# Chunked attention and a squared-ReLU feed-forward on one core: stores on the GpSimd queue, loads of two groups issued ahead of them, and a first block that starts in halves

## The chip, the cores and the metric

The kernel runs on one core of a Trainium2 chip. The metric is the device time of one execution in microseconds (us). A core has five engines with instruction streams of their own: TensorE (PE in the profile; its weight loads are PEld), VectorE (DVE), ScalarE (ACT), GpSimd (POOL) and SyncE (SP). Each takes its instructions strictly in order, and a DMA is issued by an instruction on one of these streams ("SPq", "ACTq", "POOLq" in the profile), so a DMA that must wait holds up everything behind it on that engine.

## The reference

Queries, keys and values have the shape 8 batches x 8 heads x 576 tokens x 64. Attention is computed inside chunks of 64 tokens; its output, laid out as 4608 tokens x 512, goes through a feed-forward with 2048 hidden units.

```
scores = scale * q_c @ k_c^T                   # within each chunk of 64 tokens
attn   = exp(scores - max) / (sum + 1e-9)
x      = (attn @ v_c) as [4608, 512]           # heads side by side
h      = maximum(x @ w_in, 0)                  # [4608, 2048]
out    = (h * h) @ w_out                       # [4608, 512], float32
```

## The kernel before

**Groups and blocks.** The 4608 tokens form 18 groups of 256 tokens; two groups make a block of 512. The blocks are [0, 1], [3, 2], [4, 5], ..., [16, 17] (line 41). The feed-forward works through a block at a time, and the attention of later groups is woven into it.

**One block of feed-forward.** `ffn_in` (L305) runs over 16 tiles `ft` of 128 hidden units. For each it makes four matmuls into a PSUM bank of the ring `ps_ffn` (four banks, L52), a ReLU on ACT (L318) and a square on DVE (L319) into `gT`. `ffn_out` (L323) then makes, for each of four tiles of 128 tokens, 16 matmuls into a `ps_ffn` bank, copies the bank to `o_sb` on ACT (L345) and stores 256 KB to `out` (L346). Block 0 uses `ffn_out_by_ft` (L350) instead, which takes hidden tiles in the outer loop so that it can follow the arrival of `w_out`; its stores are at L373. The very last tile is stored in two halves by ACT and SP (L340).

**Attention of one group**, by the names in the plan: the transposes of q and k (on PE through PSUM for groups 0 to 3: T, and TE for the first two; from group 4 on a cast to bf16 on POOL, C, L216, followed by a DMA transpose on SP's queue, TD, L223); the scores and their exponential (SC, L237 and L244); the product with the values and the division (AV, L260, L267, L268); and the transpose of the result to `xT`, which feeds `ffn_in` (XT: on PE for groups under 6, L287 and L291, by DMA on SP's queue after that, L281). SC, AV, XT and the PE transposes take their PSUM from the ring `ps_att` (two tiles of two banks each, L53). In T, q and k share one such tile: DVE copies the q half, ACT the k half (L173).

**The order is written out by hand.** The schedule is manual: each engine executes its instructions in the order of the program text. Each block has a table of slots (L411 to L445). A slot is one `yield` of `ffn_in` (one `ft`) or of `ffn_out` (four `ft`). At a slot, one piece of the coming loads may be issued on SP, and then the steps planned for it. A slot places an instruction between others of its own engine; it is not a point in time. Loads of q and k are at L102 and L110, of v at L117 and L124, of the weights at L136 and L144 (five staging buffers, each freed by a cast on POOL, L139 and L147). All of them run on SP's queue, but for the first `w_in` load, which ACT issues. A DMA on SP or ACT takes a completion semaphore out of a small rotating set, and waits until the earlier DMA on that semaphore has landed.

**The start** (L382 to L399). After the loads of groups 0 and 1 the order on PE is: transposes of 0, scores of 0, transposes of 1, values of 0, scores of 1, `xT` of 0, values of 1, `xT` of 1, with 46 filler matmuls in between (`keep_busy`, L207). Then come the weight loads and the loads of groups 3 and 2, and block 0's `ffn_in` over all 512 columns.

**Blocks 0 to 2.** Block 0 issues no loads in its slots (L417). Block 1 issues the loads of groups 4 and 5 in slots 0 to 16, then C of 4 and 5 at slots 22 and 26, TD at 27 and 31, then the q and k loads of groups 6 and 7 from slot 34; the scores of 4 and 5 are at slot 37. After the last slot of block 1, C and TD of groups 6 and 7 follow (L457 to L460). Block 2 makes the scores of 6 and 7 at slot 6, and block 3 those of 8 and 9 at slot 8.

Of the kernel before, what the change touches and what calls it, by code (L numbers as in the profile page):

```python
# [17 lines left out]
def kernel(  # L18
# [9 lines left out]
    nc = tc.nc  # L28
# [143 lines left out]
        for t in range(2):  # L172
            copy(out=dst[:, t], in_=src[:, t])  # L173

    def transpose_qk(g):
        ps = ps_att.tile([128, 1024], FP32, name="ps_att").bitcast(BF16)
        qkT = att_pool.tile([128, 2, 2, n_hp, 128], BF16, name="qkT", bufs=4)
        state["qkT", g] = qkT
        for which in range(2):
            transpose_paired(g, which, ps[:, which * 1024:(which + 1) * 1024])  # L180
        for which, copy in enumerate((nc.vector.tensor_copy, nc.scalar.copy)):
            copy_paired(copy, qkT[:, which], ps[:, which * 1024:(which + 1) * 1024])

    def transpose_qk_early(g, k_copy):
        qkT = att_pool.tile([128, 2, 2, n_hp, 128], BF16, name="qkT", bufs=4)
        state["qkT", g] = qkT
        for which, copy in enumerate((nc.vector.tensor_copy, k_copy)):
            bank = ps_ffn.tile([128, 512], FP32, name="ps_ffn").bitcast(BF16)
            transpose_paired(g, which, bank)
            copy_paired(copy, qkT[:, which], bank)  # L190

# [52 lines left out]
        nc.scalar.activation(  # L244
            out=e.rearrange("p a h t q -> p (a h t q)"), in_=ps, func=AF.Exp, scale=scale)

    def values(g):
        e = state.pop(("e", g))
        veb = v_even[g % NV].bitcast(BF16)
        vob = [v_odd[(2 * g + n) % NO].bitcast(BF16) for n in range(3)]  # L250
        x = att_pool.tile([128, 2, n_hp, 2, D], BF16, name="x", bufs=3)
        state["x", g] = x
        for t in range(2):
            ps = ps_att.tile([128, 2, 512], FP32, name="ps_att")
            for hp in range(n_hp):
                for a in range(2):
                    for p in range(2):
                        c = p ^ a
                        vb = vob[t + p] if a else veb[:, t]
                        nc.tensor.matmul(  # L260
                            out=ps[64 * p:64 * p + 64, a, hp * (D + 1):(hp + 1) * (D + 1)],
                            lhsT=e[64 * c:64 * c + 64, a, hp, t, :],
                            rhs=vb[64 * c:64 * c + 64, hp, 1::2],
                            start=True, stop=True)
            o = ps[:, :, 0:n_hp * (D + 1)].rearrange("p a (h d) -> p a h d", d=D + 1)
            rec = att_pool.tile([128, 2, n_hp], FP32, name="rec", bufs=4)
            nc.vector.reciprocal(out=rec, in_=o[:, :, :, D])  # L267
            nc.vector.tensor_tensor(  # L268
                out=x[:, t].rearrange("p h a d -> p a h d"),
                in0=o[:, :, :, 0:D],  # L270
                in1=rec.to_broadcast([128, 2, n_hp, D]),
                op=ALU.mult)
# [17 lines left out]
                    identity=ident)  # L290
        nc.vector.tensor_copy(out=dst, in_=psb)  # L291

    T, C, TD = transpose_qk, cast_qk, transpose_qk_dma
    SC, AV, XT = scores, values, transpose_x

    def TE(g):
        transpose_qk_early(g, nc.scalar.copy)

    def XE(g):
        for t in range(2):  # L300
            transpose_x_early(g, t)

    gTs = {}

    def ffn_in(j, c, n):  # L305
        if j not in gTs:
            gTs[j] = ffn_pool.tile([128, n_ft, BT], BF16, name="gT")
        gT, xT = gTs[j], xTs[j]
        for ft in range(n_ft):
            h = ps_ffn.tile([128, 512], FP32, name="ps_ffn")  # L310
            for dt in range(n_dt):
                nc.tensor.matmul(  # L312
                    out=h[:, 0:n],
                    lhsT=w_in_bf[:, dt, ft * 128:(ft + 1) * 128],
                    rhs=xT[:, c // 128:(c + n) // 128, dt, :],
                    start=(dt == 0), stop=(dt == n_dt - 1))
            rl = ffn_pool.tile([128, 512], BF16, name="rl", bufs=3)
            nc.scalar.activation(out=rl[:, 0:n], in_=h[:, 0:n], func=AF.Relu)  # L318
            nc.vector.tensor_tensor(  # L319
                out=gT[:, ft, c:c + n], in0=rl[:, 0:n], in1=rl[:, 0:n], op=ALU.mult)  # L320
            yield

    def ffn_out(j):  # L323
        gT = gTs.pop(j)
        for tt in range(len(blocks[j]) * GT // 128):
            o_ps = ps_ffn.tile([128, d_model], FP32, name="ps_ffn")
            for ft in range(n_ft):
                nc.tensor.matmul(  # L328
                    out=o_ps,
                    lhsT=gT[:, ft, tt * 128:(tt + 1) * 128],  # L330
                    rhs=w_out_bf[:, ft, :],
                    start=(ft == 0), stop=(ft == n_ft - 1))
                if ft == n_ft - 1:
                    t0 = blocks[j][tt // 2] * GT + tt % 2 * 128
                    if j == len(blocks) - 1 and tt == 2 * len(blocks[j]) - 1:
                        for copy, dma, c in ((nc.scalar.copy, nc.scalar, 0),
                                             (nc.vector.tensor_copy, nc.sync, 256)):
                            o_sb = ffn_pool.tile([128, d_model], FP32, name="o_sb", bufs=4)
                            copy(out=o_sb[:, 0:256], in_=o_ps[:, c:c + 256])
                            dma.dma_start(  # L340
                                out=out[t0:t0 + 128, c:c + 256], in_=o_sb[:, 0:256])
                        yield
                        continue
                    o_sb = ffn_pool.tile([128, d_model], FP32, name="o_sb", bufs=4)
                    nc.scalar.copy(out=o_sb, in_=o_ps)  # L345
                    nc.scalar.dma_start(out=out[t0:t0 + 128, :], in_=o_sb)  # L346
                if ft % 4 == 3:
                    yield

    def ffn_out_by_ft(j):  # L350

        gT = gTs.pop(j)
        n_tt = len(blocks[j]) * GT // 128
        o_ps = [ps_ffn.tile([128, d_model], FP32, name="ps_ffn") for _ in range(n_tt)]

        def mm(tt, ft):
            nc.tensor.matmul(  # L357
                out=o_ps[tt],
                lhsT=gT[:, ft, tt * 128:(tt + 1) * 128],
                rhs=w_out_bf[:, ft, :],  # L360
                start=(ft == 0), stop=(ft == n_ft - 1))

        for ft in range(n_ft - 4):
            for tt in range(n_tt):
                mm(tt, ft)
            yield
        for tt in range(n_tt):
            for ft in range(n_ft - 4, n_ft):
                mm(tt, ft)
            o_sb = ffn_pool.tile([128, d_model], FP32, name="o_sb", bufs=4)  # L370
            nc.scalar.copy(out=o_sb, in_=o_ps[tt])
            t0 = blocks[j][tt // 2] * GT + tt % 2 * 128
            nc.scalar.dma_start(out=out[t0:t0 + 128, :], in_=o_sb)  # L373
            yield

    def pieces(grps):
# [3 lines left out]
            yield from v_pieces(g)  # L380

    go(pieces([0, 1]))  # L382
    transpose_qk_early(0, nc.scalar.copy)
    keep_busy(8)
    SC(0)
    keep_busy(6)
    transpose_qk_early(1, nc.scalar.copy)
    load_w_in(0, nc.scalar, 2)
    AV(0)
    SC(1)  # L390
    keep_busy(8)
    XE(0)
    keep_busy(8)
    AV(1)
    keep_busy(8)
    transpose_x_early(1, 0)
    keep_busy(4)
    transpose_x_early(1, 1)
    keep_busy(4)  # L399

    for i in range(1, 8):
        load_w_in(i)
# [5 lines left out]
    for j, grps in enumerate(blocks):  # L408
# [5 lines left out]
            plan.setdefault(slot, []).append((f, g))  # L414

        if j == 0:
            loads, go_slots = iter(()), []  # L417
            for slot, f in ((24, T), (27, SC), (29, AV), (31, XT)):
                at(slot, f, nxt[0])
            at(31, T, nxt[1])  # L420
            phases = [ffn_in(0, 0, 512), ffn_out_by_ft(0)]
        elif j == 1:
            go_slots = [*range(17), *range(34, 48)]
            loads = itertools.chain(pieces(nxt), *map(qk_pieces, far))
            for slot, f in ((4, SC), (8, AV), (12, XT)):
                at(slot, f, grps[1])
            for i, g in enumerate(nxt):
                for slot, f in ((22 + 4 * i, C), (27 + 4 * i, TD), (37, SC), (39 + 2 * i, AV),
                                (42 + 2 * i, XT)):
                    at(slot, f, g)  # L430
            phases = [ffn_in(1, 0, 256), ffn_in(1, 256, 256), ffn_out(1)]
        else:
            loads, go_slots = pieces(far), range(32)
            slots = {SC: 8, AV: 11, XT: 15, C: 14, TD: 19}
            if j == 2:
                loads = itertools.chain(*map(v_pieces, nxt), loads)
                slots = {SC: 6, AV: 11, XT: 14, C: 20, TD: 24}
# [4 lines left out]
            for i, g in enumerate(far):  # L442
                at(slots[C] + 2 * i, C, g)
                at(slots[TD] + 3 * i, TD, g)
            phases = [ffn_in(j, 0, len(grps) * GT), ffn_out(j)]  # L445
        slot = 0
        for phase in phases:
            for _ in phase:
# [42 lines left out]
```

The softmax here doesn't subtract the row's maximum and nothing guards it: scores larger than these inputs give would overflow.

## Time and profile before

| | |
|---|---|
| five runs, us | 298.38, 302.17, 299.77, 296.31, 300.91 |
| their median, us | 299.77 |
| the profiled execution, us | 298.72 |
| its span, first to last instruction, us | 296.9 |
| PE busy in the span | 281.6 us (95%) |
| ACT, DVE, POOL busy | 130.9, 115.2, 49.5 us |
| mean granted TensorE clock | 0.993 |
| DMA | 57.04 MB, 192 GB/s over the span |

The span leaves out 1.8 us of the profiled execution's own time. A wait is listed with the engine and line that waited, and then with what released it: "PE ps_att L237 <- DMA qkT<-qkb" is the scores waiting for a DMA transpose. In a timeline, a row's first number is its start, the second its length.

### The profile page before, as it was taken

The page shows a single profiled execution, that of the slowest core. Times are in us where ns is not written, and L with a number is a line of the kernel's source. Part 1 is how long each engine was busy: PE and PEld are TensorE (multiplying, and loading weights), DVE is VectorE, ACT ScalarE, POOL GpSimd, SP SyncE. Part 2 cuts the span into 40 slices and gives each one's busy share as a digit, 9 for nine tenths or more (in the row PEclk, how much of TensorE's full clock was granted, in tenths as well). Part 3 has the DMA queues.
Part 4 walks back from the last instruction along what each step waited for, and adds up shares of the span by engine and source line. Part 5 has one row for each costly group of instructions (what it writes and reads, how often), then busy time and mean ns, then how long its engine had stood idle before and what let it go on. Part 6 is the DMA issues. An engine that isn't in the chain of part 4 may idle for free.

```text
span 296.9 us, 6372 instructions
## 1 busy us (share of the span) xinstructions
PE 281.6 (95%) x2590; PEld 141.5 (48%) x2590; DVE 115.2 (39%) x247; ACT 130.9 (44%) x225; POOL 49.5 (17%) x68
## 2 busy tenths in 40 slices
PE   2799999899998999999999999999999999999995
PEld 1664445776454444444444444444444444444442
DVE  1247903684335620553046405630662046205400
ACT  1436505665327611761167126712771177127511
POOL 2047830050032022023004003200320000000000
PEclk9979999999999999999999999999999999999999
DMA  7999999999998999999999999689968601311011
GB/s 204 247 328 361 372 280 212 274 199 190 236 226 202 203 206 246 220 205 212 245 251 204 190 266 237 135 136 290 252 142 153 163 38 24 84 71 39 0 71 71
DMA packets 158381, 57.04 MB, mean 192 GB/s; under 512 B 139280, under 2 KB 151824, under 8 KB 158352
## 3 DMA queue, kind: packets, MB, share of 16 engines
q1 hardware_dynamic: 152640, 46.81, 76.1%
q10 hardware_dynamic: 5712, 9.83, 10.1%
q8 instruction: 20, 0.33, 0.5%
q14 instruction: 9, 0.07, 0.1%
HBM read 36.70 MB, written 9.44 MB: 155 GB/s over the span
## 4 chain that ended last, share of the span: by engine, by line
PE 80%; DMA 9%; SPq 5%; DVE 2%; POOL 1%; issue 1%; ACT 1%; POOLq 0%
PE ps_ffn L312 37%; PE ps_ffn L328 34%; PE ps_ffn L357 5%; DMA qkT<-qkb 5%; DMA q_sb<-in_q_dram 3%; DMA w_st<-in_moe_w_in_dram 2%; PE ps_att L260 2%; SPq L124 2%; PE ps_att L237 2%; SPq L102 1%; SPq L117 1%; PE ps_att L164 1%; SPq L223 1%; DVE gT L319 1%; POOL qkb L216 1%
## 5 line engine op out<-in xcount | busy, mean ns | idle before, releaser
L312 PE MATMUL ps_ffn<-xT,w_in_bf 128*128 128x512 bf16 (+1 forms) x640 | 128.9, 358 | 1.9 <-ACT rl L318 1.0
L319 DVE TENSOR_TENSOR gT<-rl 128x512 bf16<-128x512 bf16 (+1 forms) x160 | 77.2, 500 | 129.6 <-ACT rl L318 127.1
L328 PE MATMUL ps_ffn<-w_out_bf,gT 128*128 128x512 bf16 x512 | 112.7, 379 | 0.0
L318 ACT ACTIVATE rl<-ps_ffn 128x512 bf16<-128x512 f32 (+1 forms) x160 | 87.1, 557 | 38.5 <-PE ps_ffn L312 34.7
L312 PEld LDWEIGHTS <-w_in_bf 128*128 128x128 bf16 x640 | 61.2, 98 | 61.9 <-issue 1.1
L328 PEld LDWEIGHTS <-gT 128*128 128x128 bf16 x512 | 49.3, 98 | 58.0
L345 ACT COPY o_sb<-ps_ffn 128x512 f32<-128x512 f32 x31 | 18.2, 586 | 91.2 <-PE ps_ffn L328 82.2
L216 POOL CAST qkb<-q_sb 128x1024 bf16<-128x1024 f32 x14 | 14.8, 1057 | 144.4 <-DMA q_sb<-in_q_dram 124.6
L268 DVE TENSOR_TENSOR x<-ps_att,rec 128x512 bf16<-128x512 f32 x36 | 24.9, 692 | 1.2
L244 ACT ACTIVATE e<-ps_att 128x1024 bf16<-128x1024 f32 x18 | 17.9, 1023 | 5.4 <-PE ps_att L237 5.4
L216 POOL CAST qkb<-k_sb 128x1024 bf16<-128x1024 f32 x14 | 15.9, 1136 | 3.3 <-DMA k_sb<-in_k_dram 3.0
L357 PE MATMUL ps_ffn<-w_out_bf,gT 128*128 128x512 bf16 x64 | 14.7, 379 | 0.0
L267 DVE RECIPROCAL rec<-ps_att 128x8 f32<-128x8 f32 x36 | 7.2, 200 | 14.0 <-PE ps_att L260 14.0
L139 POOL CAST w_in_bf<-w_st 128x1024 bf16<-128x1024 f32 (+1 forms) x9 | 8.8, 979 | 18.9 <-DMA w_st<-in_moe_w_in_dram 18.9
L260 PEld LDWEIGHTS <-e 64*64 64x64 bf16 x576 | 6.9, 109 | 9.3 <-ACT rl L318 2.3
L260 PE MATMUL ps_att<-vo_sb,e 64*64 64x65 bf16 x288 | 9.2, 199 | 1.9 <-DMA vo_sb<-in_v_dram 1.9
L237 PE MATMUL ps_att<-qkT 64*64 64x64 bf16 x576 | 7.7, 197 | 2.2 <-DMA qkT<-qkb 2.2
L357 PEld LDWEIGHTS <-gT 128*128 128x128 bf16 x64 | 6.0, 98 | 7.2 <-issue 0.3
L260 PE MATMUL ps_att<-ve_sb,e 64*64 64x65 bf16 x288 | 9.1, 199 | 0.0
L147 POOL CAST w_out_bf<-w_st 128x1024 bf16<-128x1024 f32 x8 | 8.8, 1095 | 2.0 <-DMA w_st<-in_moe_w_out_dram 1.9
L237 PEld LDWEIGHTS <-qkT 64*64 64x64 bf16 x576 | 6.0, 110 | 6.4 <-issue 3.4
L173 ACT COPY qkT<-ps_att 128x512 bf16<-128x512 bf16 x4 | 2.1, 588 | 12.1 <-DVE qkT L173 10.0
(31 smaller groups left out, 47.6 us busy)
## 6 DMA issues: line engine op xcount, KB each, us to landing
out_dram<-o_sb ACTq DMA_DIRECT2D x35, 256.0 KB, 3.4
q_sb<-in_q_dram SPq DMA_DIRECT2D x25, 256.0 KB, 5.1
k_sb<-in_k_dram SPq DMA_DIRECT2D x25, 256.0 KB, 4.9
ve_sb<-in_v_dram SPq DMA_DIRECT2D x32, 128.0 KB, 3.6
vo_sb<-in_v_dram SPq DMA_DIRECT2D x32, 128.0 KB, 3.4
w_st<-in_moe_w_out_dram SPq DMA_DIRECT2D x8, 512.0 KB, 5.7
w_st<-in_moe_w_in_dram SPq DMA_DIRECT2D x7, 512.0 KB, 6.9
q_sb<-in_q_dram SPq DMA_DIRECT2D x3, 512.0 KB, 6.7
```

The costliest lines, as they stand in the source:

```text
L139: nc.gpsimd.tensor_copy(out=w_in_bf[:, :, i * 256 + c:i * 256 + c + n], in_=st[:, :, c:c + n])
L216: nc.gpsimd.tensor_copy(out=qkb[:, which], in_=qk[g][which].rearrange("p t h d -> p (t h d)"))
L237: nc.tensor.matmul(out=ps[64 * c:64 * c + 64, o0:o0 + 64], lhsT=qkT[64 * a:64 * a + 64, 1, t, hp, cols], rhs=qkT[64 * a:64 * a + 64, 0, t, ...
L244: nc.scalar.activation(out=e.rearrange("p a h t q -> p (a h t q)"), in_=ps, func=AF.Exp, scale=scale)
L260: nc.tensor.matmul(out=ps[64 * p:64 * p + 64, a, hp * (D + 1):(hp + 1) * (D + 1)], lhsT=e[64 * c:64 * c + 64, a, hp, t, :], rhs=vb[64 * c: ...
L268: nc.vector.tensor_tensor(out=x[:, t].rearrange("p h a d -> p a h d"), in0=o[:, :, :, 0:D], in1=rec.to_broadcast([128, 2, n_hp, D]), op=AL ...
L312: nc.tensor.matmul(out=h[:, 0:n], lhsT=w_in_bf[:, dt, ft * 128:(ft + 1) * 128], rhs=xT[:, c // 128:(c + n) // 128, dt, :], start=(dt == 0) ...
L318: nc.scalar.activation(out=rl[:, 0:n], in_=h[:, 0:n], func=AF.Relu)
L319: nc.vector.tensor_tensor(out=gT[:, ft, c:c + n], in0=rl[:, 0:n], in1=rl[:, 0:n], op=ALU.mult)
L328: nc.tensor.matmul(out=o_ps, lhsT=gT[:, ft, tt * 128:(tt + 1) * 128], rhs=w_out_bf[:, ft, :], start=(ft == 0), stop=(ft == n_ft - 1))
L345: nc.scalar.copy(out=o_sb, in_=o_ps)
L357: nc.tensor.matmul(out=o_ps[tt], lhsT=gT[:, ft, tt * 128:(tt + 1) * 128], rhs=w_out_bf[:, ft, :], start=(ft == 0), stop=(ft == n_ft - 1))
```

## The change

- All 35 stores at L346 and L373 are issued on POOL's queue instead of ACT's. The two half stores of the last tile stay on ACT and SP.
- The 17 load pieces of groups 4 and 5 stand in block 0's slots 0 to 16, in program order ahead of block 0's four stores; block 1 keeps the q and k pieces of groups 6 and 7, from slot 30 on.
- At the start the scores of group 1 come ahead of the values of group 0; the values of group 1 and the `xT` transposes of group 0 alternate tile by tile; 34 filler matmuls remain, all of them ahead of the first `xT` transpose. `ffn_in` of block 0 makes its first four hidden tiles in two halves of 256 columns, and the first two tiles of the first half are put around the `xT` transposes of group 1.
- The PE transposes of groups 3 and 2 take a PSUM tile each for q and k: two of `ps_att` for group 3 (TA), one of `ps_att` and one `ps_ffn` bank for group 2 (TM).
- Block 0's plan is shifted by two slots (its phases have 34 slots instead of 32, because of the four tiles made in halves and the two made ahead of the loop, so the steps keep their places in the feed-forward). In block 1, AV of group 2 moves from slot 8 to 7, C of groups 4 and 5 from 22 and 26 to 16 and 20, TD from 27 and 31 to 21 and 25. In block 3, SC moves from slot 8 to 9.

```diff
-        for ft in range(n_ft):
+        for c, n, ft in ((c, n, ft) for c, n, fts in parts for ft in fts):
             h = ps_ffn.tile([128, 512], FP32, name="ps_ffn")
...
-                    nc.scalar.dma_start(out=out[t0:t0 + 128, :], in_=o_sb)
+                    nc.gpsimd.dma_start(out=out[t0:t0 + 128, :], in_=o_sb)
...
-            nc.scalar.dma_start(out=out[t0:t0 + 128, :], in_=o_sb)
+            nc.gpsimd.dma_start(out=out[t0:t0 + 128, :], in_=o_sb)
...
-    transpose_qk_early(0, nc.scalar.copy)
+    TE(0)
     keep_busy(8)
     SC(0)
     keep_busy(6)
-    transpose_qk_early(1, nc.scalar.copy)
+    TE(1)
     load_w_in(0, nc.scalar, 2)
+    keep_busy(8)
+    SC(1)
+    keep_busy(4)
     AV(0)
-    SC(1)
     keep_busy(8)
-    XE(0)
-    keep_busy(8)
-    AV(1)
-    keep_busy(8)
+    transpose_x_early(0, 0)
+    AV(1, [0])
+    transpose_x_early(0, 1)
+    AV(1, [1])
+    n_early = 4
+    early = ffn_in(0, [(0, 256, range(n_early)), (256, 256, range(n_early)),
+                       (0, 512, range(n_early, n_ft))])
+    next(early)
     transpose_x_early(1, 0)
-    keep_busy(4)
+    next(early)
     transpose_x_early(1, 1)
-    keep_busy(4)
...
         if j == 0:
-            loads, go_slots = iter(()), []
-            for slot, f in ((24, T), (27, SC), (29, AV), (31, XT)):
+            loads, go_slots = pieces(far), range(17)
+            for slot, f in ((26, TA), (29, SC), (31, AV), (33, XT)):
                 at(slot, f, nxt[0])
-            at(31, T, nxt[1])
-            phases = [ffn_in(0, 0, 512), ffn_out_by_ft(0)]
+            at(33, TM, nxt[1])
+            phases = [early, ffn_out_by_ft(0)]
         elif j == 1:
-            go_slots = [*range(17), *range(34, 48)]
-            loads = itertools.chain(pieces(nxt), *map(qk_pieces, far))
-            for slot, f in ((4, SC), (8, AV), (12, XT)):
+            loads, go_slots = itertools.chain(*map(qk_pieces, far)), range(30, 48)
+            for slot, f in ((4, SC), (7, AV), (12, XT)):
                 at(slot, f, grps[1])
             for i, g in enumerate(nxt):
-                for slot, f in ((22 + 4 * i, C), (27 + 4 * i, TD), (37, SC), (39 + 2 * i, AV),
+                for slot, f in ((16 + 4 * i, C), (21 + 4 * i, TD), (37, SC), (39 + 2 * i, AV),
                                 (42 + 2 * i, XT)):
                     at(slot, f, g)
...
-            slots = {SC: 8, AV: 11, XT: 15, C: 14, TD: 19}
+            slots = {SC: 9 if j == 3 else 8, AV: 11, XT: 15, C: 14, TD: 19}
```

More of the change, by code (lines that the diff above doesn't have):

```diff
@@ L173, in copy_paired, with transpose_qk @@
             copy(out=dst[:, t], in_=src[:, t])
-    def transpose_qk(g):
-        ps = ps_att.tile([128, 1024], FP32, name="ps_att").bitcast(BF16)
+    def transpose_qk(g, q_pool, k_pool):
         qkT = att_pool.tile([128, 2, 2, n_hp, 128], BF16, name="qkT", bufs=4)
         state["qkT", g] = qkT
[L179 to L188, printed above, removed]
+        for which, pool in enumerate((q_pool, k_pool)):
+            copy = nc.scalar.copy if which else nc.vector.tensor_copy
+            if pool is ps_ffn:
+                bank = pool.tile([128, 512], FP32, name="ps_ffn")
+            else:
+                bank = pool.tile([128, 1024], FP32, name="ps_att")
+            bank = bank.bitcast(BF16)[:, 0:1024]
             transpose_paired(g, which, bank)
@@ L245, in scores, with values @@
             out=e.rearrange("p a h t q -> p (a h t q)"), in_=ps, func=AF.Exp, scale=scale)
-    def values(g):
-        e = state.pop(("e", g))
+    def values(g, tiles=(0, 1)):
+        e = state["e", g]
         veb = v_even[g % NV].bitcast(BF16)
         vob = [v_odd[(2 * g + n) % NO].bitcast(BF16) for n in range(3)]
-        x = att_pool.tile([128, 2, n_hp, 2, D], BF16, name="x", bufs=3)
-        state["x", g] = x
-        for t in range(2):
+        if 0 in tiles:
+            state["x", g] = att_pool.tile([128, 2, n_hp, 2, D], BF16, name="x", bufs=3)
+        x = state["x", g]
+        for t in tiles:
             ps = ps_att.tile([128, 2, 512], FP32, name="ps_att")
@@ L291, in transpose_x, with TA, TM @@
         nc.vector.tensor_copy(out=dst, in_=psb)
-    T, C, TD = transpose_qk, cast_qk, transpose_qk_dma
+    C, TD = cast_qk, transpose_qk_dma
     SC, AV, XT = scores, values, transpose_x
+    def TA(g):
+        transpose_qk(g, ps_att, ps_att)
     def TE(g):
-        transpose_qk_early(g, nc.scalar.copy)
+        transpose_qk(g, ps_ffn, ps_ffn)
+    def TM(g):
+        transpose_qk(g, ps_att, ps_ffn)
     def XE(g):
@@ L303, with ffn_in @@
     gTs = {}
-    def ffn_in(j, c, n):
+    def ffn_in(j, parts):
         if j not in gTs:
@@ L416 @@
         if j == 0:
-            loads, go_slots = iter(()), []
-            for slot, f in ((24, T), (27, SC), (29, AV), (31, XT)):
+            loads, go_slots = pieces(far), range(17)
+            for slot, f in ((26, TA), (29, SC), (31, AV), (33, XT)):
                 at(slot, f, nxt[0])
-            at(31, T, nxt[1])
-            phases = [ffn_in(0, 0, 512), ffn_out_by_ft(0)]
+            at(33, TM, nxt[1])
+            phases = [early, ffn_out_by_ft(0)]
         elif j == 1:
-            go_slots = [*range(17), *range(34, 48)]
-            loads = itertools.chain(pieces(nxt), *map(qk_pieces, far))
-            for slot, f in ((4, SC), (8, AV), (12, XT)):
+            loads, go_slots = itertools.chain(*map(qk_pieces, far)), range(30, 48)
+            for slot, f in ((4, SC), (7, AV), (12, XT)):
                 at(slot, f, grps[1])
             for i, g in enumerate(nxt):
-                for slot, f in ((22 + 4 * i, C), (27 + 4 * i, TD), (37, SC), (39 + 2 * i, AV),
+                for slot, f in ((16 + 4 * i, C), (21 + 4 * i, TD), (37, SC), (39 + 2 * i, AV),
                                 (42 + 2 * i, XT)):
                     at(slot, f, g)
-            phases = [ffn_in(1, 0, 256), ffn_in(1, 256, 256), ffn_out(1)]
+            phases = [ffn_in(1, [(0, 256, range(n_ft)), (256, 256, range(n_ft))]), ffn_out(1)]
         else:
             loads, go_slots = pieces(far), range(32)
-            slots = {SC: 8, AV: 11, XT: 15, C: 14, TD: 19}
+            slots = {SC: 9 if j == 3 else 8, AV: 11, XT: 15, C: 14, TD: 19}
             if j == 2:
@@ L444 @@
                 at(slots[TD] + 3 * i, TD, g)
-            phases = [ffn_in(j, 0, len(grps) * GT), ffn_out(j)]
+            phases = [ffn_in(j, [(0, BT, range(n_ft))]), ffn_out(j)]
         slot = 0
```

## The prediction, made before the result was known

> **What bounds the kernel.** I read the shares of busy time first, then PE by stretches, then what PE waits for. The stretches below are: the start in three parts, the first half of block 1, and everything from block 4 on (columns: PE, PEld, DVE, ACT, POOL busy with instruction counts, granted clock, DMA share, GB/s).
>
> ```profile
> 12.60:16.00 3.40, 1.78 (x74) 1.46 (x75) 1.92 (x5) 1.51 (x3) 0.00 (x0) 1.00 1.16 264
> 16.00:19.40 3.40, 3.12 (x54) 2.72 (x55) 2.01 (x5) 0.74 (x2) 1.17 (x2) 0.51 1.00 305
> 19.40:20.80 1.40, 1.02 (x18) 0.87 (x16) 0.55 (x2) 0.59 (x1) 1.04 (x1) 0.98 1.09 375
> ...
> 52.50:69.90 17.40, 15.87 (x204) 13.37 (x201) 13.15 (x37) 12.61 (x34) 4.52 (x4) 1.00 0.98 229
> ...
> 147.00:293.40 146.40, 146.39 (x1158) 67.15 (x1156) 51.77 (x112) 65.66 (x108) 13.27 (x12) 1.00 0.68 144
> ```
>
> PE is the bound: from 147 on it is never idle, and nothing there can be won without removing matmuls. What is left is the 20.78 us before the feed-forward starts, the tail behind 293.43, and PE's waits between. These are, by PE's list of waits for 50 to 130 us:
>
> ```profile
> PE ps_att L237 <- DMA qkT<-qkb: 2.2, 3, 1.2
> PE ps_ffn L312 <- ACT rl L318: 1.0, 1, 1.0
> PE ps_ffn L312 <- DVE xT L291: 0.5, 1, 0.5
> ```
>
> In the timeline they lie at 55.42 (0.97, ACT), 62.97 (0.54, `xT`), 75.87 (0.18), 94.32 (0.82) and 126.75 (1.16, all three a transposed q and k): together 3.67 us, the whole stock that this change can draw on in mid-kernel.
>
> **The start.** The feed-forward starts at 20.78. The listed releaser is the cast of the second `w_in` piece, 19.70 to 20.74, but hidden tile 0 needs only the first piece, cast by 18.79; what it waits for is the last `xT` copy on DVE (20.21 + 0.42 = 20.63). The change needs only group 0's columns for the first tiles. I place the steps by their rows: values of group 1 still wait for a v load that lands at 18.0, so hidden tiles 0 and 1 of the first half run between 18.4 and 20.7. Tile 2 waits for the second `w_in` cast, 20.74, as its load is not moved. So eight matmuls of 256 columns, 0.117 us each (16 in 1.87 in the chain), are done by then: -0.94. The 32 half matmuls cost 32 x 0.117 = 3.74 where 16 whole ones cost 16 x 0.2175 = 3.48: +0.26. ACT and DVE get four more pieces each, about 0.7 us, below PE's pace. Sum -0.68, from -0.9 to +0.4 with the clock: half clock filled 16.0 to 19.4 after a stretch in which PE was busy 1.78 of 3.40 us; a stretch with 3.12 busy was followed by full clock. The Trainium skill (TensorE: Matmul & The Clock Gate, Part 1) has the same window, about 3.4 us, and by it the change's fillers speak against it: of 46, the 24 behind group 0's first `xT` transpose go, and 12 new ones stand earlier. I count 2.1 us of fillers out of that stretch (8 in 1.06, 8 in 1.04), and some 0.9 of group 0's transposes and 0.9 to 1.7 of early tiles at half clock in: 2.8 to 3.6 of 3.4 us. So I keep full clock; by the rule's other outcome the two us after 20.8 run at half rate and cost 1.0, giving +0.3. Scores of group 1 moved ahead are worth nothing themselves: the values behind them wait for v at 14.5 either way.
>
> **Transposes of group 2 (TM), -0.97.** The ACT copy of k waits for DVE's copy of q because they share a tile: DVE runs 52.63 to 53.92, ACT 54.00 to 55.07, then the first ReLU, and PE has filled its four banks. With a tile each, ACT can start once the transposes end at 52.6 and is done by 53.8, so the fifth tile's bank is free near 54.2, when PE asks at 54.4. The k bank costs one of four `ps_ffn` banks until 53.8; the fourth tile asks at 53.95. TA needs both `ps_att` tiles; q's copy ends at 45.28 and the scores come at 46.57, so 1.3 us cover it.
>
> **AV one slot earlier, -0.25.** The 0.54 wait is DVE-bound: after the division four squares (1.64 us) stand ahead of the `xT` copy, and moving AV by one slot (0.47) puts a fifth square (0.4) there. I take half; ends 0 and -0.54.
>
> **Loads ahead of the stores.** SP's own waits have this line, and its timeline these:
>
> ```profile
> SPq L110 <- DMA out_dram<-o_sb: 3.9, 2, 3.0
> ```
> ```profile
> 49.87 0.39 SPq L124 DMA_DIRECT2D vo_sb<-in_v_dram  x1
> 53.32 0.37 SPq L110 DMA_DIRECT2D q_sb<-in_q_dram  x1
> 54.52 0.37 SPq L110 DMA_DIRECT2D k_sb<-in_k_dram  x1
> ```
>
> Group 4's first loads wait for block 0's stores to land. The Trainium skill (DMA: Bandwidth & Descriptors, Issuing engines are not separate DMA queues) says that another issuing engine only saves issue time, since all share 16 DMA engines; by it this is worth 0. By the row, SP gets back up to 3.9 us. Both hold in part: DMA is at a share of 1.0 or more here, but fell to 0.70 at 62 to 64. I take 3.5 us earlier for all 17 loads and the DMA transposes behind them. C and TD of groups 4 and 5 gain nothing from their slots: POOL stood idle 19.0 us for q's landing. The scores' wait at 75.87 goes: -0.18, with 3 us to spare. Sum so far -0.68 - 0.97 - 0.25 - 0.18 = -2.08: block 1 ends at 87.08 - 2.08 = 85.0.
>
> **Stores on POOL: where the stall goes.** ACT loses 35 issues of 0.34 us; it stands idle 82 us for PE ahead of its copies, so this is worth 0. POOL gets 35 issues. In blocks 0 and 2 to 8 it has time: casts are waiting for loads for 14 to 20 us, and where a cast holds a store (block 2, up to 7 us) four `o_sb` buffers cover a block of 29 us. But C of groups 6 and 7 stands in the text behind block 1's last store. Before:
>
> ```profile
> 83.78 1.04 POOL L216 CAST qkb<-q_sb 128x1024 bf16<-128x1024 f32 x1 [16.67 <-DMA q_sb<-in_q_dram]
> ...
> 87.12 0.59 ACT L345 COPY o_sb<-ps_ffn 128x512 f32<-128x512 f32 x1 [3.31 <-DMA out_dram<-o_sb]
> ...
> 88.36 1.04 POOL L216 CAST qkb<-q_sb 128x1024 bf16<-128x1024 f32 x1 [2.55 <-DMA q_sb<-in_q_dram]
> 89.34 1.23 POOL L216 CAST qkb<-k_sb 128x1024 bf16<-128x1024 f32 x1
> ...
> 94.32 0.44 PE L237 MATMUL ps_att<-qkT 64*64 64x64 bf16 x32 [0.82 <-DMA qkT<-qkb]
> ```
>
> The first cast ran 3.3 us before that copy even started. Now it must follow copy and store. From the end of block 1's matmuls, E: copy 0.69 with its hand-over, the store on POOL s, four casts 4.4 (1.04 to 1.23 each), then the DMA transpose of group 7, 3.7 from issue to landing (90.60 to 94.27; others up to 5.2), hand-over 0.1: scores at E + 8.9 + s. No row shows a POOL issue: ACT's takes 0.34; the Trainium skill (DMA: Bandwidth & Descriptors) gives about 1 us to the first byte of a POOL DMA (Latency and other measured facts) and a fixed 2.0 in all (Anatomy of one DMA). I take s = 1.0, as POOL's software makes the descriptors (its smallest cast here, 0.61, is the nearest row): ends 0.35 and 2.0. So E + 9.9, where before it was 94.32 - 87.08 = E + 7.24: **+2.66** (from +2.0 to +5). PE reaches these scores at E + 6.4, so it waits about 3.5 us, in two parts, for groups 6 and 7. The loads' lead of 3.5 us is lost here: SP too waits for these casts, its v loads and all of groups 8 and 9 standing behind TD; it goes on at about 92.7 instead of 92.25.
>
> **Block 3.** PE is 0.58 late after that (-2.08 + 2.66). The DMA transpose of group 9 lands about 0.5 late, 127.2. One slot (0.87) of feed-forward now comes ahead of the scores: PE asks at 125.59 + 0.58 + 0.87 = 127.04 and waits 0.2 instead of 1.16: -0.96. The values, at slot 11, are still two slots (1.7 us) behind a 1.02 us exponential.
>
> **Sum.** -2.08 + 2.66 - 0.96 = -0.38. Blocks 4 to 8 have no waits, and the last tile's stores are unchanged, so the end follows. The profiled execution, span 296.9 and 1.8 around it, would go from 298.72 to 298.3. The median of the runs is 1.05 above it: 299.77 - 0.38 = **299.4 us**.
>
> **Rivals.** *The casts come in time* (faster). If POOL is passed quickly and the DMA transposes are short on a free queue, the wait in block 2 vanishes with the one in block 3: -2.08 - 0.82 - 1.16 = -4.06, 295.7 us. For it: loads of 6 and 7 land by 85, and POOL idles. Against it: the order on POOL and 4.4 us of casts. It needs 3.5 us less between E and the scores.
>
> *A store holds POOL until it has landed* (slower). The stores land 3.3 us after issue (median, 1.7 to 5.9), so s is about 4.0: +3.0. PE then idles 6.5 us around the scores of block 2, longer than a clock stretch, and 3.4 us at half clock add 1.7: -0.38 + 4.7 = +4.3, 304.1 us. Beyond s = 1.4 the change loses. For it: no row shows POOL's issue. Against it: ACT goes on 0.34 after issuing.
>
> *The clock alone drops* at my own stall of 3.5 us: +1.7, 301.1 us. Stalls of 1.2 did not do it.
>
> *The loads are not earlier*, as SP waits for its own landings instead. Only the 0.18 is lost, since POOL decides block 2: 299.6, and I count it into the forecast.
>
> **Chances.** Forecast 0.50 (own range 297.5 to 301.2), casts in time 0.25, POOL held 0.15, clock 0.10. A measurement here tells about 1% from no change, 3 us, as the five runs differ by 2%. Faster by over 1%: 0.22 + 0.03 = 0.25; slower by over 1%: 0.14 + 0.03 + 0.03 = 0.20; within: 0.55. Low 295.2 leaves out under half of the fast case, high 303.5 two thirds of the slow one, 0.2 in all.
>
> **What would show it.** Right: ReLU wait at 55 gone; SP's first load of group 4 near 48 to 50; POOL's cast of group 6 directly behind block 1's last store, and PE waiting over 2 us for `qkT` in block 2; no wait over 0.4 in block 3. Wrong: a PE clock of 0.5 behind 19.4, casts of group 6 ahead of that store, a store on POOL much over 1 us, or new waits from block 4 on.

## The result, and the profile after

| | before | changed |
|---|---|---|
| median of the runs, us | 299.74 (79 runs) | 301.56 (44 runs) |
| profiled execution, us | 298.72 | 301.57 |
| its span, us | 296.9 | 299.8 |
| end of PE's last matmul, by the last copies, us | 293.43 | 295.97 |
| mean granted clock of the profiled execution | 0.993 | 0.983 |

The ratio of changed to before is 1.0091, 95% interval [1.0075, 1.0107]: 0.9% slower, where I had forecast a gain of 0.1%. The time lies in the forecast range, and the direction was wrong. (Ratios leave disturbed runs out, and they are taken against runs of the kernel before on the same chips; the medians of the kernel before on three chips differ by up to 1.3 us.)

PE's waits between 50 and 130 us, in the profile after:

```profile
PE ps_att L233 <- DMA qkT<-qkb: 2.9, 2, 1.6
PE ps_ffn L315 <- DVE xT L288: 1.0, 1, 1.0
```

The 0.97 us wait for the ReLU is gone, the one for `xT` has doubled, and the waits for `qkT` are two instead of three, and longer. Where they lie, with what POOL does ahead of them, in the timeline after:

```profile
86.85 0.59 ACT L348 COPY o_sb<-ps_ffn 128x512 f32<-128x512 f32 x1 [3.31 <-PE ps_ffn L331]
...
87.73 0.54 POOL L349 DMA_DIRECT2D out_dram<-o_sb  x1 [3.36 <-ACT o_sb L348]
88.27 1.05 POOL L212 CAST qkb<-q_sb 128x1024 bf16<-128x1024 f32 x1
89.25 1.05 POOL L212 CAST qkb<-k_sb 128x1024 bf16<-128x1024 f32 x1
...
90.23 1.04 POOL L212 CAST qkb<-q_sb 128x1024 bf16<-128x1024 f32 x1
...
91.21 1.03 POOL L212 CAST qkb<-k_sb 128x1024 bf16<-128x1024 f32 x1
...
94.18 0.45 PE L233 MATMUL ps_att<-qkT 64*64 64x64 bf16 x32 [1.32 <-DMA qkT<-qkb]
...
96.22 0.65 PE L233 MATMUL ps_att<-qkT 64*64 64x64 bf16 x32 [1.59 <-DMA qkT<-qkb]
```

POOL waits for the copy, issues block 1's last store, and only then makes the four casts, with no gap: the order in which they stand. PE then stops twice for the scores of groups 6 and 7.

What the prediction had not put into its sum is in the clock (the column ahead of the DMA share). First the start, then block 2 around and behind the two waits; the last row is the kernel before around its own wait in block 2:

```profile
13.95:17.36 3.41, 2.05 (x51) 1.52 (x50) 2.26 (x5) 0.77 (x2) 0.00 (x0) 1.00 1.14 310
17.36:20.77 3.41, 2.30 (x24) 1.75 (x25) 1.81 (x5) 0.76 (x2) 2.05 (x3) 0.50 1.11 349
20.77:24.19 3.42, 3.42 (x20) 2.52 (x18) 2.77 (x5) 1.36 (x4) 2.23 (x3) 0.50 1.08 347
```
```profile
92.39:95.87 3.48, 0.92 (x35) 0.33 (x32) 2.52 (x7) 3.08 (x5) 0.00 (x0) 1.00 1.11 249
95.87:99.28 3.41, 3.06 (x38) 1.40 (x39) 0.00 (x0) 1.58 (x2) 0.00 (x0) 0.50 0.41 90
```
```profile
92.39:95.87 3.48, 2.66 (x74) 1.38 (x73) 0.95 (x3) 3.06 (x5) 0.00 (x0) 1.00 0.86 194
```

Half clock holds for two stretches of 3.4 us at the start, the second of them full of feed-forward matmuls, and for one behind a stretch in which PE was busy 0.92 of 3.48 us. Each full stretch at half clock costs up to 1.7 us.

To place the whole, I set the feed-forward's progress in the two profiled executions side by side: when each has streamed the same number of columns through PE. The table has the change of the lag in each stage, as forecast and as measured, and the lag at the stage's end, all in us; a minus is a lead of the changed kernel.

| stage | change forecast | change measured | lag at its end |
|---|---|---|---|
| start and block 0 | -0.68 | +0.96 | +0.96 |
| block 1: transposes of group 2 | -0.97 | -1.18 | -0.22 |
| block 1: `xT` of group 2 | -0.25 | +0.28 | +0.06 |
| block 1: its output half | -0.18 | -0.33 | -0.27 |
| block 2 | +2.66 | +3.58 | +3.31 |
| block 3 | -0.96 | -0.62 | +2.69 |
| blocks 4 to 8 | 0 | -0.14 | +2.55 |

### The profile page after: what moved, and what is told of

It reads as the page before. It is cut to its first block, busy times and chain, and to the rows that moved or that the text cites. A ratio compares the mean times of both kernels' runs of the same rounds, so it can differ in the third digit from the quotient of the medians.

```text
span 299.8 us, 6398 instructions
## 1 busy us (share of the span) xinstructions
PE 282.6 (94%) x2594; PEld 142.5 (48%) x2594; DVE 120.3 (40%) x251; ACT 131.3 (44%) x229; POOL 67.8 (23%) x103
## 4 chain that ended last, share of the span: by engine, by line
PE 85%; DMA 5%; DVE 3%; issue 2%; POOL 1%; ACT 1%; SPq 0%; POOLq 0%; ACTq 0%
PE ps_ffn L315 38%; PE ps_ffn L331 36%; PE ps_ffn L360 5%; DMA w_st<-in_moe_w_in_dram 2%; DMA k_sb<-in_k_dram 2%; PE ps_att L233 2%; PE ps_att L257 2%; DVE gT L322 2%; DMA qkT<-qkb 1%; POOL qkb L212 1%; DVE x L265 1%; PE ps_ffn L164 1%; ACT rl L321 1%; PE ps_ffn L206 1%; PE ps_att L164 1%
## 5 line engine op out<-in xcount | busy, mean ns | idle before, releaser
L322 DVE TENSOR_TENSOR gT<-rl 128x512 bf16<-128x512 bf16 (+1 forms) x164 | 82.6, 521 | 127.5 <-ACT rl L321 124.5
L315 PE MATMUL ps_ffn<-xT,w_in_bf 128*128 128x512 bf16 (+1 forms) x656 | 132.6, 360 | 1.1 <-DVE xT L288 1.0
L315 PEld LDWEIGHTS <-w_in_bf 128*128 128x128 bf16 x656 | 64.1, 100 | 61.1 <-issue 1.6
L349 POOL DMA_DIRECT2D out_dram<-o_sb x31 | 16.7, 540 | 152.2 <-ACT o_sb L348 152.2
```

The costliest lines, as they stand in the source:

```text
L315: nc.tensor.matmul(out=h[:, 0:n], lhsT=w_in_bf[:, dt, ft * 128:(ft + 1) * 128], rhs=xT[:, c // 128:(c + n) // 128, dt, :], start=(dt == 0) ...
L322: nc.vector.tensor_tensor(out=gT[:, ft, c:c + n], in0=rl[:, 0:n], in1=rl[:, 0:n], op=ALU.mult)
L349: nc.gpsimd.dma_start(out=out[t0:t0 + 128, :], in_=o_sb)
```

## The experiments

In the diffs, "changed" is the kernel after the change. Percentages are against the kernel before.

**1. The casts ahead of the store** (changed; the casts move to slot 44, ahead of block 1's last store).

```diff
+            for g in far:
+                at(44, C, g)
...
             for g in far:
-                C(g)
                 TD(g)
```

> Changed kernel, but POOL's casts of groups 6 and 7 stand ahead of block 1's last store instead of behind it. Theory P (the order on POOL makes the stall, and the stall makes the clock drop): the casts run about 3.5 us earlier, PE's two waits for qkT in block 2 (1.32 and 1.59) shrink to under 1 us together, no half-clock stretch follows at 96, and the time falls by 3 to 4 us, to about 298 (0.5% under the kernel before). Theory D (stores on POOL or earlier loads slow the DMA transposes and the loads of 6 and 7 themselves): the waits stay above 2 us and the time above 300.5.

Measured: 297.7 us (12 runs), ratio 0.9963 [0.9927, 0.9999]. In its profile the first cast starts at 85.14 instead of 88.27, no wait for `qkT` is left between 30 and 130 us, and there is no half clock from 20 us to the last matmul. This execution also had full clock at the start, so the fair measure is block 2 alone: the lag falls by 0.83 us there, where it grows by 3.58 in the changed kernel. Theory P holds; theory D falls.

**2. One store back on ACT** (changed, a single instruction on another queue).

```diff
-                    nc.gpsimd.dma_start(out=out[t0:t0 + 128, :], in_=o_sb)
+                    eng = nc.scalar if j == 1 and tt == 3 else nc.gpsimd
+                    eng.dma_start(out=out[t0:t0 + 128, :], in_=o_sb)
```

> Changed kernel with one store of the 35, block 1's last, back on ACT's queue; nothing else differs. Theory P: this one store holds the casts of groups 6 and 7, so they start as their loads land, about 4 us earlier; PE's waits for qkT in block 2 fall from 2.9 to under 1 us and the time by 3 to 4 us, to the 297.6 of the kernel with the casts first. Rival (POOL's 35 stores cost as a sum, or slow DVE and DMA): the time falls by less than 1 us.

Measured: 297.16 us (6 runs), ratio 0.9895 [0.9845, 0.9944] (the two medians on that chip, 297.16 and 299.44, give 0.992). Its timeline:

```profile
83.72 0.54 POOL L350 DMA_DIRECT2D out_dram<-o_sb  x1 [4.49 <-DMA q_sb<-in_q_dram]
84.25 1.05 POOL L212 CAST qkb<-q_sb 128x1024 bf16<-128x1024 f32 x1
...
92.68 0.95 PE L233 MATMUL ps_att<-qkT 64*64 64x64 bf16 x64
```

The first cast starts at 84.25 instead of 88.27, PE makes both groups' scores in one piece, and the lag falls by 0.76 us in block 2. This is the plainest proof of the cause: 34 stores on POOL cost nothing that shows, and the 35th costs over 1% of the time, through the casts that stand behind it.

**3. The stores alone** (kernel before, its 35 stores on POOL, at L346 and L373).

> Kernel before, with only the 35 stores moved to POOL's queue. Theory P: this part alone carries the whole loss, as POOL casts groups 6 and 7 behind block 1's last store: PE's waits for qkT in block 2 grow from 0.8 to about 2.9, half clock follows in block 2, and the time rises by 2.5 to 3.5 us (0.8 to 1.2%). Rival (the store queue is harmless without the other parts): within 0.3% of the kernel before.

Measured: 301.81 us (12 runs), ratio 1.0055 [1.0021, 1.0089]. The waits are those of the changed kernel:

```profile
95.00 0.45 PE L237 MATMUL ps_att<-qkT 64*64 64x64 bf16 x32 [1.34 <-DMA qkT<-qkb]
...
97.09 0.45 PE L237 MATMUL ps_att<-qkT 64*64 64x64 bf16 x32 [1.64 <-DMA qkT<-qkb]
```

In this execution the clock stayed full behind them, so block 2's lag grew by 2.24 us: the stall without the clock's share. In block 3 the kernel before waits 1.16 us for a transposed k; this wait is gone here, and the lag falls from 2.77 to 1.60. So the order on POOL slows this kernel as well, by less than the 0.8% expected in the middle of the runs; their interval reaches 0.89%, so whether the stores alone carry the whole loss of 0.91% is not settled.

**4. All stores back on ACT** (changed, both lines).

> Changed kernel with all stores back on ACT's queue; loads, start and all else stay as changed. Theory P: the casts of 6 and 7 start as their loads land, the waits in block 2 fall from 2.9 to under 1.2 us, no half clock at 96, time down 2.5 to 3.5 us, to about 298.5. Theory D': the store's queue does not matter and SP is late anyway, so block 2 still waits over 2 us: time within 1 us of the changed kernel. If loads of later groups wait for ACT's stores, SP shows such waits again.

Measured: 299.26 us (12 runs), ratio 1.0012 [0.9972, 1.0052], 0.8 us above theory P's figure. Block 2 has no wait over 1 us, but block 1 has one, with half clock behind it (79.09 to 82.51); block 1's lag grows by 2.6 us:

```profile
78.18 0.45 PE L233 MATMUL ps_att<-qkT 64*64 64x64 bf16 x32 [2.54 <-DMA qkT<-qkb]
```

SP's waits show "DMA out_dram<-o_sb: 4.7, 2, 3.3" again at the loads: ACT's stores hold the loads even though these stand ahead of them in part. So the move to POOL does remove a real wait. With all stores but one on POOL (run 2) the ratio is 0.9895, with all on ACT 1.0012; the one store that holds the casts turns the gain into a loss.

**5. PE kept busy while it waits in block 2** (changed; the fillers write into the score tile ahead of the scores).

```diff
+        for _ in range({6: 22, 7: 26}.get(g, 0)):
+            nc.tensor.matmul(out=ps[:, 0:128], lhsT=ident, rhs=ident, start=True, stop=True)
```

> Changed kernel, with 22 and 26 filler matmuls written into the score tiles of groups 6 and 7 ahead of their scores, so that PE is busy where it waits in block 2; the waits for qkT stay. Theory K (of the 3.6 us lost in block 2, 2.1 are the stall and 1.5 the half clock behind it): no half clock near 96 to 99, time down 1.2 to 1.5 us, to about 300.2. Rival (the clock drop has nothing to do with this idle time): half clock stays and the time is the same or up to 0.5 us longer.

Measured: 301.03 us (12 runs), ratio 1.0052 [1.0027, 1.0077], 0.4% under the changed kernel's 1.0091; the mean clock of its runs is 0.994 instead of 0.985. The intervals touch at the edges, so 1.2 us is a size, not a sharp value. The median is higher than the 300.2 expected, on a chip where the kernel before is slower too. In its profile no half clock is left in block 2, as theory K says, but the second scores come later than in the changed kernel:

```profile
94.52 0.45 PE L235 MATMUL ps_att<-qkT 64*64 64x64 bf16 x32
94.89 1.62 PE L227 MATMUL ps_att<-ident 128*128 128x128 bf16 x26
98.30 0.45 PE L235 MATMUL ps_att<-qkT 64*64 64x64 bf16 x32 [1.78 <-DMA qkT<-qkb]
```

Group 7's DMA transpose took 5.7 us from issue to landing, where it took 3.9 in the changed kernel. So this execution's lag grew by 3.95 us in block 2, all of it stall. Whether the fillers had a part in the late landing, one profile can't tell.

**6. The old start** (changed, with the order and the 46 fillers of before, block 0's hidden tiles whole).

> Changed kernel with the start of the kernel before: the old order, 46 fillers, block 0's hidden tiles whole; everything else of the change stays. Theory C (the new start costs through the clock: half clock from 17.4 to 24.2): full clock returns by about 19.5 in most runs, block 0 is 1.2 us earlier, and the time falls by about 1.2 us, to 300.3. Rival (the halves themselves are worth 0.7 us and the clock falls at random in either start): the time rises by 0 to 0.7 us.

Measured: 301.46 us (12 runs), ratio 1.0079 [1.0045, 1.0113]: no difference from the changed kernel that these runs can tell. Full clock did return before the feed-forward (at 17.99), and the lag at the end of block 0 was 0.29 instead of 0.96. Theory C's 1.2 us (0.4%) did not show in the median, but the interval just includes it.

**7. More fillers at the start** (changed, three times `keep_busy(8)` around the values of group 1).

```diff
     transpose_x_early(0, 0)
+    keep_busy(8)
     AV(1, [0])
+    keep_busy(8)
     transpose_x_early(0, 1)
+    keep_busy(8)
     AV(1, [1])
```

> Changed kernel with 24 more filler matmuls around the values of group 1, where PE waits for v loads. Theory C (idle PE before 19.4 holds the clock at half): no half clock behind 20.8, block 0's tile 8 is reached 1.7 us earlier, and the time falls by 1 to 1.9 us, to about 300. Rival (the clock isn't set by what PE does in this stretch): the half-clock stretch stays, and the fillers add 0 to 0.7 us.

Measured: 302.51 us (6 runs), ratio 1.0121 [1.0074, 1.0167]. The mechanism works: no half clock at the start, and the 24th feed-forward matmul (counted in 512 columns) starts at 25.42 instead of 26.92. The gain then dies in block 0's tail:

```profile
42.66 0.64 PE L164 MATMUL ps_att<-ident,q_sb 128*64 128x128 bf16 x16 [0.26 <-DMA q_sb<-in_q_dram]
44.38 0.64 PE L164 MATMUL ps_att<-ident,k_sb 128*64 128x128 bf16 x16 [1.08 <-DMA k_sb<-in_k_dram]
```

Behind these transposes of group 3 the lag is +1.08 again, about the changed kernel's own. Run 1, which by chance had full clock at the start and led by 0.86 us, waited 1.77 and 0.93 us at the same place. An early start is lost there: group 3's loads stand behind all the weights on SP, and its k landed at 44.34 here and 45.16 in run 1, later than the 43.27 of the kernel before. Why so late is not shown. This execution also loses 5.53 us in block 2: its waits there are 3.8 us together, and half clock follows for two stretches (96.01 to 102.84).

**8. The new start alone** (kernel before with that part only).

> Kernel before, with only the new start (scores of 1 first, values and transposes alternating, 34 fillers, four hidden tiles of block 0 in halves). Theory G (block 0's tail asks for group 3's k just as it lands, near 43.3, so a start that is earlier gains nothing, and one that is later by the clock loses its excess): time within -0.1 and +0.4% of the kernel before, and PE's lead at block 0's end is zero or negative whatever it is at tile 8. My prediction's step (-0.68 kept to the end) would give -0.2%.

Measured: 298.69 us (12 runs), ratio 0.9944 [0.9913, 0.9976]. That misses theory G on time, and is more than my own step gives. In its profile, which ends only 0.32 us ahead of the kernel before, block 0 ends 0.29 us late, and the gain appears in block 2, where the loads of groups 6 and 7 land earlier and the wait of 0.82 is absent. I can't say why they do; runs 6 and 9, which compare the two starts in other company, show no such gain.

**9. Casts first and the old start** (runs 1 and 6 in one).

> Changed kernel with both mends: POOL's casts of groups 6 and 7 ahead of block 1's last store, and the start of the kernel before. By the offsets of the single runs: 3.3 us won in block 2 and 0 to 1 us at the start, so 297 to 298 us, 0.3 to 0.7% below the kernel before; no qkT wait over 1 us in block 2. If the start matters by itself it comes out under the run with the casts alone by more than 0.7 us.

Measured: 297.9 us (12 runs), ratio 0.9944 [0.9907, 0.9981]; one wait for `qkT`, 0.55. It agrees with run 1 within both intervals: with the casts in place, which start is used does not show.

**10. Casts first, values of group 2 at slot 8.**

```diff
-            for slot, f in ((4, SC), (7, AV), (12, XT)):
+            for slot, f in ((4, SC), (8, AV), (12, XT)):
```

> Changed kernel with the casts of groups 6 and 7 ahead of block 1's last store, and the values of group 2 back at slot 8 of block 1. If the move to slot 7 is what made PE's wait for xT longer (0.54 before, 0.77 to 1.41 in kernels with it), that wait is about 0.5 again and the time 0 to 0.5 us under the run with the casts alone; if the wait is set by DVE's sum of work up to the xT copy, it stays at 0.8 to 1.0 with the same time.

Measured: 297.0 us (11 runs), ratio 0.9914 [0.9880, 0.9948]. PE still waits 1.11 us at the second half of block 1 (its listed releaser is the ReLU), so the slot alone is not what set it.

**11. The new start and the separate PSUM tiles** (kernel before with these two).

> Kernel before with the new start and the separate PSUM tiles for q and k (TA, TM); stores on ACT, loads and slots as before. Separate tiles alone: PE's wait for ACT at 55 (0.98) gone and 1.0 to 1.1 us won at the end of block 1, of which the waits for qkT in blocks 2 and 3 may take back up to all. If nothing is taken back: 0.9% under the kernel before, with the 0.56% of the new start in it; if the loads set the later blocks, within 0.2% of the run with the new start alone.

Measured: 298.28 us (12 runs), ratio 0.9961 [0.9929, 0.9992]. The wait for ACT is gone, but a wait of 1.02 for `qkT` stands in block 1's output half. Separate tiles win 1.2 us in their stage, and none of it shows beside run 8's ratio: in the profile, the next transposed q and k takes 0.84 us back.

Runs 2 and 10 are the best kernels of the study, 0.9 to 1% under the kernel before, 1.7 to 2% under the changed one; their intervals overlap.

## Why the prediction was wrong, step by step

Two terms of the clock were put at nothing: half clock behind the stall in block 2, which cost 1.4 us there in the profile after, and half clock at the start, where -0.68 was forecast and +0.96 measured. The forecast stall itself came, and where it was put. Without these two misses the stages measured in the profile would sum to about -0.5 us, near the forecast -0.38.

**The stall in block 2: mechanism right, size a little high.** The copy and its hand-over took 0.9 us where I had 0.69, the store on POOL 0.54 instead of 1.0, the casts 4.0 instead of 4.4, and the last DMA transpose 3.9 instead of 3.7. PE's second scores came at E + 9.4, with E = 86.8, where I had E + 9.9. So the stall is +2.2 and not +2.66, as run 3 also has it. Runs 1 and 2 show that this order on POOL is the cause.

**The clock behind that stall: the step that failed.** "The clock alone drops at my own stall of 3.5 us: +1.7, 301.1 us" stood as a rival with a chance of 0.10, "Stalls of 1.2 did not do it" being the reason. But the sum predicts its own stall: 0.4 us of work in 3.5. It would have been consistent to expect the drop. The measured 301.56 is near that rival in part by luck, as the rival has the start as a gain. The profiles show the clock's share cleanly. For each of five, the table has how much later after block 1's last matmul the second scores start than in the kernel before (7.24 us), what block 2 loses in all, and the stretches of half clock in it:

| profile | scores later | block 2 loses | rest | stretches of half clock |
|---|---|---|---|---|
| run 3 | 2.24 | 2.24 | 0 | 0 |
| run 5 | 3.95 | 3.95 | 0 | 0 |
| changed | 2.16 | 3.58 | 1.4 | 1 |
| run 6 | 2.19 | 3.88 | 1.7 | 1 |
| run 7 | 3.01 | 5.53 | 2.5 | 2 |

What the stall leaves over is there only where the clock fell. Run 3 shows that it need not fall behind such a stall: counted on in steps of 3.41 us from the last change of the clock, the stretch with its first wait has PE busy for 1.76 us, against 0.92, 1.30 and 1.19 in the changed kernel and runs 6 and 7. In the times, run 5 puts the clock's share at about 1.2 us.

**"So I keep full clock" at the start: wrong.** I had counted 2.8 to 3.6 us of work for the stretch of 16.0 to 19.4 and PE was busy 1.73: the values of group 1 waited 1.35 for their v load, and nothing filled the wait. Half clock then lasted from 17.36 to 24.19, and the 24th feed-forward matmul came 1.17 late where I had 0.68 early. Among the profiles of the eight kernels with this start and without extra fillers, seven have half clock past 20.8; of the four with the old start, none. Yet the -0.68 could hardly have reached the end either: in the kernel before, block 0's tail asks for group 3's k within 0.1 us of its landing, and the leads of runs 1 and 7 were lost there. Of the changed kernel's 1.17, only 0.2 was made up. I never asked what a gain at the start would wait for next. What this start is worth in the whole time stays open: runs 6 and 9 see no difference, run 8 a gain.

**Loads ahead of the stores: smaller than put.** The first load of group 4 went out at 49.34 instead of 53.32 as forecast, but the DMA transposes behind the 17 loads only 1.3 us earlier, not 3.5 (the first two rows are the changed kernel, the last is the kernel before):

```profile
49.34 1.15 SPq L110 DMA_DIRECT2D q_sb<-in_q_dram  x1
...
67.49 5.32 SPq L219 DMA_TRANSPOSE qkT<-qkb  x2
```
```profile
68.75 5.43 SPq L223 DMA_TRANSPOSE qkT<-qkb  x2
```

The first five issues on SP are longer (1.2 to 2.2 us each, where the first three took 0.4 to 1.1 before). Of the two readings, the one by which this was worth 0 came nearer. It cost nothing in the sum, since 0.18 was all that hung on it. The loads of groups 6 and 7 had landed by 87.53 (89.00 before), and not by 85 as the fast rival needed.

**Separate tiles: right** (-1.18 for -0.97), in the stage. **`xT`: wrong sign** (+0.28 for -0.25). In the changed kernel PE came 0.4 us earlier, and the copy on DVE did not: it started at 62.29, against 62.24 in the kernel before (changed, then before):

```profile
62.29 0.68 DVE L288 COPY xT<-ps_att 128x1024 bf16<-128x1024 bf16 x1
...
63.03 7.16 PE L315 MATMUL ps_ffn<-xT,w_in_bf 128*128 128x256 bf16 x64 [1.01 <-DVE xT L288]
```
```profile
62.97 7.16 PE L312 MATMUL ps_ffn<-xT,w_in_bf 128*128 128x256 bf16 x64 [0.54 <-DVE xT L291]
```

The division did end 0.6 us earlier, but five squares stand between it and the copy instead of four, and they took 2.37 us instead of 1.73; one lasted 1.12 us, beside a cast on POOL, as one did before. The wait grew in most kernels with slot 7 and also with slot 8 (run 10), and in runs 4 and 11 it was 0.5 to 0.6, so what sets it in general stays open.

**Block 3: near** (-0.62 for -0.96). The scores no longer wait, which is -1.34 up to slot 9; a wait of 0.51 for the division in DVE's queue at 136.60, in the changed kernel's profile, gives part back.

**The sum.** Of the miss of 2.9 us between -0.38 and +2.55, the start gives 1.64, block 2's clock 1.4 less 0.5 for the smaller stall, `xT` 0.53, block 3 0.34, and the other stages -0.5. Over the 44 runs of the changed kernel, the time falls by 1.3 us for each 1% of mean clock, and that clock is 0.985 where the kernel before has 0.992 to 0.995 on three chips. By these figures about 1 us of the whole is the clock; this is an estimate, as it rests on runs that differ in more than the clock.

## What to carry to other kernels

When a DMA issue moves to an engine that also computes, list what stands behind each issue there, and let the issue wait only where nothing urgent follows: here one store of 35 decided the time. When a sum contains a PE stall as long as a clock stretch, the half clock behind it belongs into the sum and not among the rivals: here it followed three of four such stalls in block 2 that had no fillers (changed, runs 6 and 7, not run 3). And a gain counts only as far as the next transfer that lands just in time.

## What the runs showed of the hardware that I had not expected

A square on DVE takes longer while POOL casts. In the changed kernel's profile, the 96 squares of 128x512 that overlap no cast last 0.41 to 0.43 us; the 27 that overlap one by more than 0.05 us have a median of 1.03. The longest is among the seven of block 2 (durations in ns: shortest, median, longest):

```profile
L322 DVE TENSOR_TENSOR gT<-rl x7: 413/425/4186, 88.3 to 94.7; 128x512 bf16<-128x512 bf16 x7
```

With the casts ahead of the store (run 1), the same seven start as the last cast ends or later:

```profile
L322 DVE TENSOR_TENSOR gT<-rl x7: 424/425/426, 89.1 to 94.3; 128x512 bf16<-128x512 bf16 x7
```

The square of 4.19 us starts 0.08 us behind the first of the four casts in a row and ends 0.28 us behind the last; runs 3, 5, 6 and 7, with the same four casts behind the store, have one of 4.19 to 4.20 us too. ACT waited 2.6 us for DVE. It hid behind PE's stall here. A store issued on POOL occupies it for 0.54 us (539 to 679 ns in all 35), not much more than the 0.34 us on ACT.
